# A linear-attention block mixed with a gated feed-forward block, on one core: 32 bytes of space behind each buffer of the x forms and of the gate/up weights

## The chip, the cores and the metric

The kernel runs on one core of one Trainium2 chip. The metric is the device time in microseconds (us) of one execution; 2% is what counts as faster or slower.

## The reference

The input `x` has 2048 tokens of width 640. Two branches read it, and a gate per token mixes them:

```
g   = sigmoid((x * gate_w).sum(-1))
# branch A: linear attention, 32 heads of 20
q, k, v = split(x @ wqkv)
phi(t)  = where(t > 0, t + 1, exp(t)) + 1e-6
kv  = einsum("bhsd,bhse->bhde", phi(k), v);  z = phi(k).sum over tokens
a   = (phi(q) @ kv / (phi(q) . z + 1e-6)) @ wo
# branch B: gated linear unit, 640 -> 1536 -> 640
b   = (sigmoid(x @ w_gate) * (x @ w_up)) @ w_down
out = g * a + (1 - g) * b
```

All of it is float32.

## The kernel before

Every float32 operand of a product is split into a high and a low part of type float32r: ScalarE copies the source into the high part (which rounds it), and VectorE subtracts the high part from the source. A product then takes three matmuls, high by high, high by low and low by high; the helper `mm3` records them, and in the profile they stand on lines 407, 408 and 409. The helper `act` is line 420, the helper `vec2` is line 424, `vec3` line 428, and the DMAs are issued on line 364, whatever they are for.

Block products are done with seven block multiplications in place of eight, so both `x` and the weights are needed as plain blocks and as sums of blocks. These are the **forms**: of `x` the plain ones `xa`, `xb` and the sums `xt`, of the weights `wg`, `wu` and `ws`. In tile names a last `h` or `l` is the high or the low part (`xth`, `xtl`).

The program has two stages.

- **First stage** (to about 140 us): k of all tokens, in four chunks of 512 tokens, and the sums over tokens of phi(k) and `x`. The forms of `x` are 256 columns wide there and are the stationary operand; the moving operands are the k weights (`k1h`, `ksh` and others, 322 columns) and phi(k) (`pkh`, `pkl`, 320 columns, with `xnh`, `xnl` stationary). `xnh`, `xnl`, `pkh` and `pkl` have six buffers each of 2576 bytes per partition, laid out 2592 bytes apart. Forms of `x`, k weights and staging tiles lie in the pool `pa` on the right side of the memory.
- **Second stage**: the q product and the feed-forward block, once for each pair of 512-token groups, over 12 slices of the 1536 hidden columns, with the down product in between, and at the end the attention output. Here the forms of `x` are 512 columns wide and are the moving operand; the weight forms `wg` (of 2 x 640 columns), `wu` (2 x 384) and `ws` (2 x 1152), high and low in one tile, are stationary. The first pair makes the weight forms and stores them to DRAM from GpSimd's queue, the second loads them back on SP's queue. At the end of the kernel the same buffers hold forms of phi(q) (`pl`, `pq`, `pt`, `p3`).

The instructions of all engines are put in order at build time by a planner (class `Order`), which keeps estimates of when TensorE, ScalarE and VectorE come free and fills in work that is due; the queues then run in the order written. Memory is allocated by pools: `px` holds the forms of `x` (tag `x2`, ten buffers of 2 x 512 columns; tag `x3`, four of 3 x 512), `pg` the `wg` buffers (two), `pz` one `ws` buffer and ahead of it the staging tile `xz`, `pw` the other `ws`, the `wu` buffers (two), and work tiles of 512 columns (tags `t` and `c`). `pw2` lies below `pw` and has, besides its tiles, an unused tile `room` of 256 columns that fills up the side. A pool made with `reuse_waits="tile"` lets a tile that lies where older tiles lay wait for just those.

In the built program all the tiles of the second stage that are named above begin 480 bytes past a multiple of 512 bytes: their sizes are multiples of 512 bytes per partition. In the first stage the forms of `x` begin at 160 modulo 512, and the other operands lie spread: `k1h` at 160, `k1l` 192, `k2h` 224, `k2l` 256, `ksh` 288, `ksl` 352, `k5h` 416, `k5l` 192, and the six buffers of `xnh` at 288, 320, 352, 384, 416 and 448, of `pkh` at 160 to 320 in steps of 32, likewise `xnl` and `pkl`.

Of the kernel before, what the change touches and what calls it, by code (L numbers as in the profile page):

```python
# [7 lines left out]
F32 = mybir.dt.float32  # L8
F32R = mybir.dt.float32r
# [5 lines left out]
P = 128  # L15
S, D, F = 2048, 640, 1536
# [3 lines left out]
TG = 512  # L20
# [3 lines left out]
CW = 256  # L24
# [350 lines left out]
def gated_mix_kernel(ctx: ExitStack, tc: tile.TileContext, xt, xn, wk, wv, wo, wst_q, wst_f, out_t):  # L375
# [10 lines left out]
    def f32(ap):  # L386
        return ap.bitcast(F32)
# [95 lines left out]
    def m1_tile(tag, name, dt=F32, rows=P):  # L483
        return m1.tile([rows, D], dt, name=name, tag=tag, bufs=2 if tag == "ma" else 3)
# [10 lines left out]
    for _ in range(8):  # L495
        nc.tensor.matmul(wps, warm[:, :P], warm, start=True, stop=True)

    class XForms:

        def __init__(self, pool, cols):  # L500
            def pair(n, name):
                return [pool.tile([P, n, cols], F32R, name=f"x{name}{c}", tag=f"x{n}", bufs=10 if n == 2 else 4)
                        for c in "hl"]
            self.fa, self.fr, self.fb = pair(2, "a"), pair(3, "r"), pair(3, "b")
            self.ft = [pair(2, "t") for _ in range(4)]

# [271 lines left out]
    def queue_qw(u):  # L778

        raw = qs.tile([P, 2, D], F32, name="qraw", tag="qraw")  # L780
        sp.dma_start(raw, wst_q[:, u:u + 2])
        g, v = raw[:, 0], raw[:, 1]
        w = 2 * P

        def piece(i, c, src):
            n = width(src)

            def fn():
                t = qs.tile([P, 2, w], F32R, name="qp", tag="qp", bufs=2)
                split(t[:, 0, :n], t[:, 1, :n], src)  # L790
                order.then(lambda: sp.dma_start(w_dram["q", u, i][:, :, c:c + n], f32(t[:, :, :n])))
            order.add(a_cost(n), v_cost(n), fn, "qw",
                      None, kept=True)

        for i, n in enumerate((D, 3 * P, 9 * P)):
            w_dram["q", u, i] = dram.tile([P, 2, n], F32, name=f"wq{u}{i}")
        for i, src, c0 in ((0, g, 0), (1, v, w)):
            for c in range(c0, D, w):
                piece(i, c - c0, src[:, c:min(c + w, D)])
        a11, a12, a21, a22 = g[:, :w], g[:, w:2 * w], v[:, :w], v[:, w:2 * w]  # L800
        g5, v5 = g[:, 2 * w:], v[:, 2 * w:]

        def sums(part):
            if part == 0:
                add(a22, a21, a22)
                sub(a21, a11, a21)
            else:
                sub(a11, a22, a11)
                sub(a12, a12, a11)
                sub(g5, g5, v5)  # L810
        for part in range(2):
            order.add(0, 2 * v_cost(w), lambda part=part: sums(part), "qw", None, kept=True)
        for n, t in ((7, a22), (0, a11), (5, a21), (2, a12), (4, g5)):
            piece(2, n * P, t)
# [4 lines left out]
    def tok(b, side):  # L819

        pr, j = divmod(b, 4)
        return (2 * pr + side) * 4 + j
# [14 lines left out]
    def queue_xn(b):  # L837
        for n in (2 * b, 2 * b + 1):
            order.add(a_cost(D), v_cost(D), lambda n=n: split_xn(n), ("xn", b), lambda n=n: xn_st[n][1])
# [248 lines left out]
    for c in range(1, 4):  # L1088
        ck = chunks[c]
        if c == 1:  # L1090
            queue_qw(2)
        a, b = KBlock(2 * c), KBlock(2 * c + 1)
        for n in range(1, 6):
            order.need((ck, n))
            if c == 1 and n >= 3:
                order.need(("ks", (1, 0, 2)[n - 3]))
            getattr(a, f"s{n}")()
            getattr(b, f"s{n}")()
            for _ in range(({1: 1, 2: 1, 3: 1, 5: 1}, {3: 2, 4: 2, 5: 2})[c - 2].get(n, 0) if c > 1 else 0):
                order.run("qw")  # L1100
        order.need((ck, 6))
        if c == 1:
            order.need(("ks", 5))
        if c == 2:
            chunks[c + 1].load()
        elif c == 3:
            nx = [Chunk(1, i, None, i * CW, xst_v, (b12h, b12l)) for i in range(2)]
            nx[0].load()
        if c == 1:
            order.need(("xn", 1))  # L1110
        queue_xn(2 * c)
        a.s6()
        a.s7()
        a.sum_b()
        a.phi_a()
        b.s6()
        a.phi_b()
        order.need(("pk", 2 * c - 1))
        k_split(tok(2 * c, 0))
        b.s7()  # L1120
        b.sum_b()
        k_split(tok(2 * c, 1))
        if c == 3:
            order.need("qw")
            qs_cm.__exit__(None, None, None)
            pa_cm.__exit__(None, None, None)
            px_cm = tc.tile_pool(name="px", bufs=1, side="right", reuse_waits="tile")
            px = px_cm.__enter__()
            xf = XForms(px, TG)
            pg_cm = tc.tile_pool(name="pg", bufs=1, side="right", reuse_waits="tile")  # L1130
            pg = pg_cm.__enter__()
            pz_cm = tc.tile_pool(name="pz", bufs=1, side="right", reuse_waits="tile")
            pz = pz_cm.__enter__()
            z = pz.tile([P, 8, CW], F32, name="xz", tag="ws")
            z0 = m1_tile("ma", "xm")[:, :2 * CW].rearrange("p (k c) -> p k c", c=CW)
            nx[1].x = (Rows((0, 2, z0), (2, KC, z[:, 0:3])), z[:, 3:8])
            nx[1].load(((0, 0, 2), (0, 2, KC), (1, 0, KC)))
            W, WT = {}, {}

            def wg_tile():  # L1140
                return pg.tile([P, 2, D], F32R, name="wg", tag="wg", bufs=2)

            def put(n, i, t):
                WT[n, i] = t
                W[n, i] = [t[:, c] for c in range(2)]

            def store_w(n, i):

                key = n[::2] + (i,)
                w_dram[key] = dram.tile(list(WT[n, i].shape), F32, name="w%s%d%d" % key)  # L1150
                gp.dma_start(w_dram[key], f32(WT[n, i]))

            def wg_split(n, src):
                put(n, 0, wg_tile())
                split(*W[n, 0], src)
                if n[0] == "f" or n[2] == 0:
                    order.then(lambda: store_w(n, 0))
            nx[0].f = nx[1].f = xf
            put(("q", 1, 2), 0, wg_tile())
            sp.dma_start(f32(WT[("q", 1, 2), 0]), w_dram["q", 2, 0])  # L1160
        g = GTBatch(c, batches[c])
        if c > 1:
            order.need(("xn", 2 * c))
        if c == 1:
            chunks[1].store_t(1, 0)
        elif c < 3:
            chunks[c + 1].queue()
        else:
            queue_xn(7)
        for u in range(6 if c == 1 else 4):  # L1170
            g.part(u, 0, 2, ("rot", "dd", "ch", "cc")[u % 4])
            if c == 1 and u == 0:
                order.need(("xn", 2))
                chunks[1].store_t(2, 3)
                chunks[2].queue()
            if u == (c == 1):
                b.phi_a()
            if u == 1 + (c == 1):
                b.phi_b()
                order.ahead(5)  # L1180
        queue_split(2 * c + 1)
        if c < 3:
            queue_xn(2 * c + 1)
        else:
            w_stage = m1_tile("ma", "w0")
            sp.dma_start(w_stage, wst_q[:, KC - 1])
            queue_forms(nx)
        for u in range(2 * KC):
            g.part(u, 2 if u in g.ps else 0, len(g.tiles),
                   ("rot", "dd", "rot", "cc")[u % 4] if c == 3 or u < 8 else "rot")  # L1190
            order.fill()
            if u in (3, 5, 7, 9,):
                order.run("qw")
            if c == 2 and u == 9:
                queue_ls()
# [18 lines left out]
    pw = pw_cm.__enter__()  # L1214
    pw2_cm = tc.tile_pool(name="pw2", bufs=1, side="right", reuse_waits="tile")
    pw2 = pw2_cm.__enter__()

    pw2.tile([P, 2, D], F32, name="wst", tag="wst", bufs=2)
    pw2.tile([P, 2, TG], F32R, name="hf", tag="hf2")
    pw2.tile([P, 256], F32, name="room")  # L1220

    def tt(name, dt=F32, shape=(P, TG)):
        return pw.tile(list(shape), dt, name=name, tag="t", bufs=4)
# [2 lines left out]
        return pw.tile(list(shape), dt, name=name, tag="c", bufs=5)  # L1226

    def wu_tile():
        return pw.tile([P, 2, 3 * P], F32R, name="wu", tag="wu", bufs=2)

    ws_n = []

    def ws_tile():
        ws_n.append(0)
        return (pz if len(ws_n) % 2 == 0 else pw).tile([P, 2, 9 * P], F32R, name="ws", tag="ws")

    def load_form(n, i):
        t = (wg_tile, wu_tile, ws_tile)[i]()
# [1251 lines left out]
    PL, PQ, BL, OMG, MHL = {}, {}, {}, {}, {}  # L2490

    def x2_tile(name="pl", dt=F32):
        return px.tile([P, 2, TG], dt, name=name, tag="x2", bufs=10)

    def x3_tile(name, dt=F32):
        return px.tile([P, 3, TG], dt, name=name, tag="x3", bufs=4)

    def load_m(i):

# [507 lines left out]
```

## Time and profile before

| | |
|---|---|
| median of two runs | 724.53 us (724.12 and 724.94) |
| profiled execution, first to last instruction | 722.5 us |
| lying around the span, against the median | 2.0 us |
| TensorE busy, matmuls | 718.2 us (99%), 3539 |
| TensorE weight loads | 616.7 us (85%) |
| VectorE busy | 587.1 us (81%) |
| ScalarE busy | 370.0 us (51%) |
| GpSimd busy | 114.0 us (16%) |
| DMA | 191.31 MB, 265 GB/s |

The profile is of one execution, and its own time is given by the span alone. Weight loads run beside matmuls, so the two shares of TensorE don't add up. In the rows below PE is TensorE, PEld its weight loads, DVE VectorE, ACT ScalarE, POOL GpSimd and SP SyncE, which only issues DMAs. A row of a group names the line, the engine, the operation, out<-in by tile names and shapes, the count, and then busy us and mean ns of one. The duration of a matmul (389 ns for 512 columns) contains its way through the array; matmuls overlap, and the pace is the distance between two starts.

### The profile page before, as it was taken

How to read it: one execution, taken by the hardware profiler on the slowest of the kernel's cores; microseconds unless marked ns; L12 is line 12 of the kernel's file. 1: busy time of each engine (PE TensorE's matmuls, PEld its weight loads, DVE VectorE, ACT ScalarE, POOL GpSimd, SP SyncE). 2: the span in 40 equal slices, each digit the busy share in tenths (PEclk: the TensorE clock that was granted, in tenths of full speed). 3: DMA queues.
4: the chain of work that ended last, by engine and by line, in shares of the span. 5: the costliest groups of instructions: out<-in, count | busy, mean ns of one | idle time of the engine just before them, and what ended most of it. 6: DMA issues, size and time to landing. Idle time of an engine off the chain costs nothing.

```text
span 722.5 us, 10190 instructions
## 1 busy us (share of the span) xinstructions
PE 718.2 (99%) x3539; PEld 616.7 (85%) x3539; DVE 587.1 (81%) x1028; ACT 370.0 (51%) x686; POOL 114.0 (16%) x184
## 2 busy tenths in 40 slices
PE   9999999999999999999999999999999999999998
PEld 8999999988888888888888888888888888888886
DVE  6898888988677989898989977447696968799895
ACT  6884748367556654545364664354423242454451
POOL 0211112113311212111210224001010101002200
PEclk9999999999999999999999999999999999999999
DMA  7677689598787866757687899968989895959947
GB/s 258 162 230 182 179 196 286 129 357 280 273 303 259 325 241 234 262 221 264 244 321 273 255 313 360 404 222 292 364 256 309 247 395 182 407 217 332 217 101 240
DMA packets 81690, 191.31 MB, mean 265 GB/s; under 512 B 12154, under 2 KB 40202, under 8 KB 77926
## 3 DMA queue, kind: packets, MB, share of 16 engines
q1 hardware_dynamic: 60726, 117.72, 49.6%
q0 software_dynamic: 20624, 72.70, 30.2%
q8 instruction: 28, 0.46, 0.3%
q10 hardware_dynamic: 288, 0.23, 0.1%
q14 instruction: 24, 0.20, 0.1%
HBM read 113.14 MB, written 75.20 MB: 261 GB/s over the span
## 4 chain that ended last, share of the span: by engine, by line
PE 99%; DMA 0%; DVE 0%; ACT 0%; issue 0%
PE ch L407 11%; PE ch L409 11%; PE ch L408 11%; PE cc L409 9%; PE cc L407 9%; PE cc L408 9%; PE dd L407 7%; PE dd L408 7%; PE dd L409 7%; PE rot L407 5%; PE rot L408 5%; PE rot L409 5%; PE rot L1578 1%; PE dd L2735 1%; PE ch L2735 0%; DMA xnh<-wk 0%
## 5 line engine op out<-in xcount | busy, mean ns | idle before, releaser
L420 ACT ACTIVATE c<-ch 128x512 f32<-128x512 f32 x54 | 32.3, 597 | 84.2 <-PE ch L409 83.4
L424 DVE TENSOR_TENSOR hf<-c,hf 128x512 fp32r<-128x512 f32 x80 | 54.4, 687 | 19.3 <-ACT hf L420 18.9
L420 ACT ACTIVATE hf<-c 128x512 fp32r<-128x512 f32 x80 | 48.9, 624 | 31.1 <-DVE c L424 31.0
L424 DVE TENSOR_TENSOR c<-cc,c 128x512 f32<-128x512 f32 x42 | 28.9, 688 | 28.3 <-PE cc L409 17.4
L407 PE MATMUL ch<-xth,ws 128*128 128x512 f32 x112 | 43.6, 389 | 0.0
L408 PE MATMUL ch<-xtl,ws 128*128 128x512 f32 x112 | 43.6, 389 | 0.0
L409 PE MATMUL ch<-xth,ws 128*128 128x512 f32 x112 | 43.6, 389 | 0.0
L424 DVE TENSOR_TENSOR c<-c,c 128x512 f32<-128x512 f32 x52 | 35.7, 687 | 3.3 <-ACT c L420 2.7
L424 DVE TENSOR_TENSOR tb<-rot,tb 128x512 f32<-128x512 f32 x56 | 36.1, 682 | 0.3 <-PE rot L409 0.3
L407 PE MATMUL dd<-xrh,wg 128*128 128x512 f32 x90 | 35.2, 391 | 0.0
L408 PE MATMUL dd<-xrl,wg 128*128 128x512 f32 x90 | 35.1, 390 | 0.0
L409 PE MATMUL dd<-xrh,wg 128*128 128x512 f32 x90 | 35.0, 389 | 0.0
L420 ACT ACTIVATE c<-dd 128x512 f32<-128x512 f32 x22 | 13.1, 596 | 41.4 <-PE dd L409 41.4
L407 PE MATMUL cc<-xbh,ws 128*128 128x512 f32 x84 | 32.7, 389 | 0.0
L408 PE MATMUL cc<-xbl,ws 128*128 128x512 f32 x84 | 32.7, 389 | 0.0
L409 PE MATMUL cc<-xbh,ws 128*128 128x512 f32 x84 | 32.7, 389 | 0.0
L424 DVE TENSOR_TENSOR tb<-dd,tb 128x512 f32<-128x512 f32 x36 | 24.7, 686 | 9.3 <-PE dd L409 9.2
L420 ACT ACTIVATE dd<-ch 128x512 f32<-128x512 f32 x22 | 12.8, 582 | 35.9 <-PE ch L409 35.9
L424 DVE TENSOR_TENSOR tb<-cc,tb 128x512 f32<-128x512 f32 x36 | 24.5, 684 | 1.9 <-PE cc L409 1.9
L424 DVE TENSOR_TENSOR wst<-wst 128x256 f32<-128x256 f32 (+1 forms) x65 | 24.6, 396 | 1.4
L409 PEld LDWEIGHTS ch<-xth,ws 128*128 128x128 f32 x112 | 21.0, 188 | 4.7 <-DVE ws L424 0.3
L408 PEld LDWEIGHTS ch<-xtl,ws 128*128 128x128 f32 x112 | 21.0, 188 | 4.3
(703 smaller groups left out, 2378.9 us busy)
## 6 DMA issues: line engine op xcount, KB each, us to landing
wf<-ws POOLq DMA_DIRECT2D x12, 1152.0 KB, 7.5
ws<-wf SPq DMA_DIRECT2D x11, 1152.0 KB, 8.8
wst<-wst_f SPq DMA_DIRECT2D x12, 640.0 KB, 4.9
wf<-wg POOLq DMA_DIRECT2D x12, 640.0 KB, 6.1
wd<-wd POOLq DMA_DIRECT2D x12, 640.0 KB, 8.1
wg<-wf SPq DMA_DIRECT2D x12, 640.0 KB, 6.9
wf<-wd SPq DMA_DIRECT2D x10, 640.0 KB, 11.0
xnst<-xn SPq DMA_DIRECT2D x16, 320.0 KB, 4.5
```

Of the source, the lines that this page charges most:

```text
L407: nc.tensor.matmul(out, l_hi, r_hi, start=first, stop=False, skip_group_check=True)
L408: nc.tensor.matmul(out, l_hi, r_lo, start=False, stop=False, skip_group_check=True)
L409: nc.tensor.matmul(out, l_lo, r_hi, start=False, stop=last, skip_group_check=True)
L420: nc.scalar.activation(out, src, fn, **kw)
L424: nc.vector.tensor_tensor(out, a, b, op=op)
L1578: nc.tensor.matmul(ps[:w, :w], v[:, m, :w], gt[:, m, c0:c0 + w], start=(m == 0), stop=(m == KC - 1))
L2735: nc.tensor.matmul(ps, l, r, start=new, stop=j == 1 and k == ks[-1], skip_group_check=True)
```

## The change

A helper `spaced` allocates a tile with 8 more columns (32 bytes) than it uses and returns a view without them. The second stage's forms of `x` (`x2`, `x3`), the weight forms `wg`, `wu` and `ws`, and the tiles that later take these buffers are allocated with it; `xz` gets the size of the `ws` that follows it. The pads take 640 bytes per partition, and `room` gives 640 back (256 to 96 columns).

```
+    def spaced(pool, n, cols, dt, name, tag, bufs, space=8):
+        t = pool.tile([P, n * cols + space], dt, name=name, tag=tag, bufs=bufs)
+        return t[:, :n * cols].rearrange("p (a b) -> p a b", a=n)
...
-                return [pool.tile([P, n, cols], F32R, name=f"x{name}{c}", tag=f"x{n}", bufs=10 if n == 2 else 4)
-                        for c in "hl"]
+                return [spaced(pool, n, cols, F32R, f"x{name}{c}", f"x{n}", 10 if n == 2 else 4,
+                               8 if cols == TG else 0) for c in "hl"]
...
-            z = pz.tile([P, 8, CW], F32, name="xz", tag="ws")
+            z = spaced(pz, 8, CW, F32, "xz", "ws", 1, 2 * 9 * P + 8 - 8 * CW)
...
-                return pg.tile([P, 2, D], F32R, name="wg", tag="wg", bufs=2)
+                return spaced(pg, 2, D, F32R, "wg", "wg", 2)
...
-    pw2.tile([P, 256], F32, name="room")
+    pw2.tile([P, 96], F32, name="room")
...
-        return pw.tile([P, 2, 3 * P], F32R, name="wu", tag="wu", bufs=2)
+        return spaced(pw, 2, 3 * P, F32R, "wu", "wu", 2)
...
-        return (pz if len(ws_n) % 2 == 0 else pw).tile([P, 2, 9 * P], F32R, name="ws", tag="ws")
+        return spaced(pz if len(ws_n) % 2 == 0 else pw, 2, 9 * P, F32R, "ws", "ws", 1)
...
-        return px.tile([P, 2, TG], dt, name=name, tag="x2", bufs=10)
+        return spaced(px, 2, TG, dt, name, "x2", 10)
...
-        return px.tile([P, 3, TG], dt, name=name, tag="x3", bufs=4)
+        return spaced(px, 3, TG, dt, name, "x3", 4)
```

Where the buffers begin, in bytes modulo 512, in the two built programs:

| buffers | before | after |
|---|---|---|
| `x2` (ten) | 480 each | 32, 64, 96 and on in steps of 32 to 320 |
| `x3` (four) | 480 each | 352, 384, 416, 448 |
| `wg` (two) | 480, 480 | 480, 0 |
| `wu` (two) | 480, 480 | 384, 416 |
| `ws` (in `pw`, in `pz`) | 480, 480 | 352, 448 |
| `t` and `c` (nine), not padded | 480 each | 448 each |
| four work tiles (tag `c2`) and one `hf`, not padded | 480 each | 352 each |

The high and the low part of one weight form lie in one tile and keep their distance; those of an `x` form lie in two buffers and now differ. Both programs have the same instructions in the same order on every engine, and the same waits but for three.

On SP's queue, near the end of the first stage, `xz` is loaded. These are the rows before (DMAHW and DMASW are semaphores of DMAs, the engines' names those of engines):

```order
L364 DMA xm<-xt 128x2x256 [waits DMAHW5_49,DVE_49]
L364 DMA xz<-xt 128x3x256 [waits DMASW7_49,DMAHW6_49,DMASW6_49,DMAHW7_49,DMASW5_49,DMASW4_49]
L364 DMA xz<-xt 128x5x256
L364 DMA wg<-wq_500 128x1280 [waits DMAHW0_49,PE_49]
L364 DMA w_1578<-wst_q 128x640 [waits DMAHW1_49,DVE_49]
```

and now:

```order
L364 DMA xm<-xt 128x2x256 [waits DMAHW5_49,DVE_49]
L364 DMA xz<-xt 128x3x256 [waits DMASW7_49,DMASW6_49,DMAHW6_49,DMASW5_49,DMAHW7_49,DMASW4_49,PE_49]
L364 DMA xz<-xt 128x5x256
L364 DMA wg<-wq_500 128x1280 [waits DMAHW0_49,PE_49]
L364 DMA w_1578<-wst_q 128x640 [waits DMAHW1_49,DVE_49]
```

The load of `xz` waits for TensorE too: the wider tile reaches over the start of the first stage's `xah`.

On ScalarE, early in the second stage, products of the q and feed-forward forms are copied out of PSUM (`ch`) into work tiles of tag `c`. Before:

```order
L420 ACTIVATE woh<-wo_sb 100x640 [waits DMAHW4_49]
L420 ACTIVATE c_2042<-ch_1851 128x512 [waits PE_49]
L420 ACTIVATE qe<-c_1859 128x512
L420 ACTIVATE c_1859<-c_1859 128x512 [waits Activation_49]
L420 ACTIVATE ms<-dd_2054 120x320 [waits PE_49]
L420 ACTIVATE ms<-dd_2061 120x320 [waits PE_49]
L420 ACTIVATE woh<-wo_sb 100x640 [waits DMAHW5_49]
L420 ACTIVATE c_2107<-ch_1851 128x512 [waits DMASW1_49,PE_49]
```

and now:

```order
L420 ACTIVATE woh<-wo_sb 100x640 [waits DMAHW4_49]
L420 ACTIVATE c_2042<-ch_1851 128x512 [waits DMASW1_49,PE_49]
L420 ACTIVATE qe<-c_1859 128x512
L420 ACTIVATE c_1859<-c_1859 128x512 [waits Activation_49]
L420 ACTIVATE ms<-dd_2054 120x320 [waits PE_49]
L420 ACTIVATE ms<-dd_2061 120x320 [waits PE_49]
L420 ACTIVATE woh<-wo_sb 100x640 [waits DMAHW5_49]
L420 ACTIVATE c_2107<-ch_1851 128x512 [waits PE_49]
```

The wait for a DMA out of the first stage's `kr` or `kb` tiles has moved from the later copy to the earlier one, since another of the `c` buffers is the first to lie over them.

## The prediction

> **What bounds the kernel now.** I read the page from the top: the share of busy time, the slices, then the chain that ended last.
>
> ```profile
> span 722.5 us, 10190 instructions
> PE 718.2 (99%) x3539; PEld 616.7 (85%) x3539; DVE 587.1 (81%) x1028; ACT 370.0 (51%) x686; POOL 114.0 (16%) x184
> PE   9999999999999999999999999999999999999998
> PEclk9999999999999999999999999999999999999999
> PE 99%; DMA 0%; DVE 0%; ACT 0%; issue 0%
> ```
>
> TensorE is busy for 718.2 of 722.5 us, in every slice, at full granted clock, and the chain is TensorE from end to end: no transfer and no other engine has a share. A busy TensorE can still run below its best pace, so the next view is the table of stretches (busy time and count of each engine):
>
> ```profile
> 0.00:20.00 20.00, 19.00 (x112) 16.43 (x113) 13.69 (x33) 12.94 (x31) 1.08 (x5) 1.00 0.80 263
> 20.00:135.00 115.00, 115.00 (x782) 115.00 (x782) 99.17 (x189) 74.21 (x150) 21.51 (x23) 1.00 0.74 196
> 135.00:200.00 65.00, 65.00 (x349) 56.33 (x349) 52.63 (x103) 40.05 (x72) 14.95 (x27) 1.00 0.85 280
> 200.00:410.00 210.00, 210.00 (x925) 172.79 (x924) 185.07 (x327) 113.71 (x209) 37.95 (x66) 1.00 0.76 272
> 410.00:700.00 290.00, 290.00 (x1280) 239.85 (x1279) 222.87 (x359) 124.50 (x220) 38.55 (x63) 1.00 0.86 288
> 700.00:722.50 22.50, 19.19 (x99) 16.28 (x97) 13.68 (x22) 4.55 (x8) 0.00 (x0) 1.00 0.67 210
> ```
>
> The only idle time of TensorE is 1.0 us in the first stretch and 3.3 us in the last (the final copy and store). The fullest neighbour is VectorE between 200 and 410 us: 185.07 of 210, that is 88%.
>
> Now the pace: the distance from one matmul's start to the next, by stretches of one width. The count of a stretch includes the two matmuls (one in the last row) that had begun before it; taking them off leaves the number of steps.
>
> ```profile
> 420.00:540.00 120.00, 120.00 (x531) 1.00 0.89 315
> 179.42:715.21 535.79, 535.79 (x2362) 1.00 0.82 280
> 80.96:98.41 17.45, 17.45 (x121) 1.00 0.77 177
> 64.96:80.81 15.85, 15.85 (x110) 1.00 0.50 131
> 715.44:718.91 3.47, 3.47 (x30) 1.00 0.47 170
> ...
> 419.99 0.39 PE L409 MATMUL cc<-xth,ws 128*128 128x512 f32 x1
> 539.90 0.39 PE L407 MATMUL cc<-xbh,wu 128*128 128x512 f32 x1
> 80.96 0.31 PE L407 MATMUL rot<-pkh,xnh 128*128 128x320 f32 x1
> 80.81 0.31 PE L409 MATMUL cc<-k5h,xbl 128*128 128x322 f32 x1
> 718.91 0.28 PE L409 MATMUL rot<-hf,wf 128*128 128x256 f32 x1
> ```
>
> From 419.99 to 539.90 are 529 steps of 512 columns: 119.91/529 = **226.7 ns**. Over the whole 512-column stretch, 535.79/2360 = 227.0 ns. The 320-column stretch of the first stage gives 17.45/119 = 146.6 ns, the 322-column one 15.85/107 = 148.1 ns, the 256-column end 3.47/29 = 119.7 ns. So the long stretch runs within 0.3 ns of its own best part: 0.3 × 2360 = 0.8 us is all that TensorE loses there to waits of any kind.
>
> **The change part by part.** No instruction is added, removed or reordered on any engine; the order rows show three waits that differ. What moves is where tiles lie. So the price has three parts: those waits, the pace of TensorE with the new starts, and the durations on VectorE, ScalarE and the DMAs.
>
> *The waits.* The load of `xz` now also waits for TensorE, because the wider tile reaches 320 bytes into where the first stage's `xah` lay. The instructions that still held that place:
>
> ```profile
> 99.91 0.19 PEld L408 LDWEIGHTS ch<-k1l,xah 128*128 128x128 f32 x1
> 115.71 1.46 SPq L364 DMA_DIRECT2D xz<-xt  x2
> 160.13 0.60 ACT L420 ACTIVATE c<-ch 128x512 f32<-128x512 f32 x1 [0.33 <-PE ch L409]
> 132.89 1.19 POOL L364 DMA_DIRECT2D zacc<-kb  x1 [3.45 <-DVE gt L424]
> zacc<-kb POOLq DMA_DIRECT2D x8, 320.0 KB, 5.5
> ```
>
> TensorE's last read of `xah` begins at 99.91 us, and the load is issued at 115.71: the wait is met long before, by up to 15.8 us. Even if it weren't, behind it on SP's queue stand the second half of `xz` and the loads of `wg`, `w0` and `wst`, and the forms made from `xz` would come late for TensorE. The DMA wait that goes from one copy to `c` (166.25 us) to an earlier one (160.13 us) is for a store out of `kr` or `kb`; the last of those is issued at 132.89 and lands 5.5 us later, 22 us ahead of the copy. Both cost 0; ScalarE's copy waits for TensorE anyway, as its row says.
>
> *VectorE and ScalarE.* The trace holds the comparison that the change makes: in the first stage the six-buffer tiles (`xnh`, `xnl`, `pkh`, `pkl`) lie 32 bytes further modulo 512 from one buffer to the next, in the second stage all lie at 480. Same operation, same 640 columns:
>
> ```profile
> L424 DVE TENSOR_TENSOR xnl<-xnst,xnh 128x640 fp32r<-128x640 f32 x15 | 11.8, 821 | 0.3
> L424 DVE TENSOR_TENSOR wg<-wst,wg 128x640 fp32r<-128x640 f32 x13 | 10.7, 821 | 5.4 <-ACT wg L420 5.4
> L424 DVE TENSOR_TENSOR wd<-dst,wd 128x640 fp32r<-128x640 f32 x12 | 9.8, 819 | 0.0
> L420 ACT ACTIVATE xnh<-xnst 128x640 fp32r<-128x640 f32 x16 | 11.1, 730 | 0.0
> L420 ACT ACTIVATE wg<-wst 128x640 fp32r<-128x640 f32 x13 | 9.5, 729 | 1.4 <-PE dd L409 1.4
> L420 ACT ACTIVATE wd<-dst 128x640 fp32r<-128x640 f32 x12 | 8.4, 727 | 0.0
> ```
>
> 821 ns spread out, 821 and 819 ns at one offset; ScalarE 730 against 729 and 727. The effect is between nothing and 0.4%, of either sign. On VectorE's 185.07 us that is 0.7 us, hidden below TensorE, which has 25 us more to do in that stretch; without that cover it would be the whole 0.7. VectorE would set the pace only if its operations grew by 13%.
>
> *TensorE.* Between the 256-column end and the 512-column stretch, both with operands at one offset, lie (226.7 − 119.7)/256 = 0.418 ns per column. This puts 320 columns at 146.4 ns and 322 at 147.3. The first stage, with its spread operands, measures 146.6 and 148.1: 0.2 and 0.8 ns more. From 135 us on there are 349 + 925 + 1280 + 99 = 2653 matmuls, so the spread costs between **0.5 and 2.1 us** if those differences are its doing. Downwards the bound is what TensorE's weight loads wait for other engines after the first 7 us:
>
> ```profile
> PEld ch L409 <- DVE ws L424: 0.3, 2, 0.2
> PEld rot L407 <- ACT rot L420: 0.3, 1, 0.3
> PEld cc L407 <- DVE tb L424: 0.2, 1, 0.2
> PEld dd L407 <- ACT dd L420: 0.2, 1, 0.2
> PEld dd L408 <- DVE xrl L424: 0.2, 1, 0.2
> PEld ch L407 <- ACT cx L420: 0.2, 1, 0.2
> ```
>
> That is 1.4 us in all, so the change is worth between −1.4 and +2.1 us here. I take 0: the 320-column stretch is the one whose tiles lie as the change lays them, in steps of 32 bytes, and its 0.2 ns is no more than the reading error of the 256-column stretch (0.01 us over 29 steps is 0.3 ns).
>
> *The DMAs.* The pads aren't transferred, so packets and bytes stay. A slower transfer would show only where an engine of the chain waits for one, and TensorE never does.
>
> **The sum.** 722.5 + 0 (waits) + 0 (VectorE, ScalarE, DMAs) + 0 (TensorE) = 722.5 us of span. The median of the two runs, 724.53, lies 2.0 us above the span; with these 2.0 the forecast is **724.5 us**, no change.
>
> **The rivals.**
> *Contention goes.* If buffers at one offset slow VectorE or ScalarE when TensorE reads beside them, spreading them takes away waits. At most 1.4 us is there to be had: 723.1. Against it: the equal rows of 640 columns. For it: VectorE's 88% leaves the 0.2 us waits as the places where a late result shows. The Trainium skill, page "SBUF — State Buffer", section "SBUF: two separate sides", says that inside the engine side only the port pair shared by VectorE and GpSimd contends; by that rule the gain is nothing and the time 724.5, and the rows of 640 columns agree.
>
> *Slower: TensorE's stream pays for its start.* The moving operands in the second stage are the forms `x2` and `x3`, and each matmul reads one from its start or from 2048 bytes on. If an operand that begins off the old common offset costs one more fetch, each of the 2653 matmuls pays; by the 322-column stretch 0.8 ns, which is 2.1 us: 726.6. It decides over the 2% only from 14.5/2653 = 5.5 ns per matmul on, seven times that price. Against it: the 320-column stretch shows 0.2. The Trainium skill, page "Advanced Engine Details and Errata", section "SBUF Cachelines", says that SBUF is read in lines of 16 bytes and that crossing lines costs. By that rule a start moved by 32 bytes costs nothing here and the time is 724.5, since every second slice of 322 columns begins 8 bytes into a line (1288 = 80 × 16 + 8) while every start of the change is a whole line; no run here separates the two.
>
> *The layout doesn't move.* The moved waits show that it does.
>
> **How the numbers follow.** Forecast (no change within the runs' spread) 0.72; contention goes 0.12; TensorE pays 0.13; something that no row shows 0.03, of it 0.01 faster and 0.02 slower by over 2%. The range takes in both rivals, with half of the 0.8 us between the two runs (724.12 and 724.94) on each side: 723.1 − 0.4 to 726.6 + 0.4, so 722.7 to 727.0. Two per cent, 14.5 us, is about what a measurement of this kernel tells from no change. Faster by more: 0.01; within: 0.97; slower by more: 0.02.
>
> **What would show it.** After the change the stretch from 420 to 540 us should again hold 531 matmuls (226.7 ns); 530 or fewer means that TensorE pays. The 640-column rows of `wg` should read 821 and 729 again, the waits of the weight loads 1.4 us in sum, the chain 99% TensorE. The forecast is wrong if the matmul pace moves by a nanosecond, if VectorE's operations grow towards 13%, or if TensorE begins to wait at `xz`'s forms near 125 us.

## The result, and the profile after

The changed kernel takes 734.91 us (734.88 and 734.95), against 724.53 us before: a ratio of 1.0142 with a 95% interval of 1.0125 to 1.0158. That is 10.4 us slower, short of the 2% and far outside the range of 722.7 to 727.0. The page after, its share of busy time, TensorE's slices and the chain that ended last:

```profile
span 733.1 us, 10190 instructions
PE 729.0 (99%) x3539; PEld 617.5 (84%) x3539; DVE 587.8 (80%) x1028; ACT 370.4 (51%) x686; POOL 114.1 (16%) x184
PE   9999999999999999999999999999999999999998
PEclk9999999999999999999999999999999999999999
PE 99%; DVE 0%; ACT 0%; issue 0%
```

This could be the page of before: the same instructions, TensorE busy for 99%, at full granted clock, alone in the chain. Only its busy time has grown, from 718.2 to 729.0 us, which is the whole difference. VectorE (587.1 to 587.8), ScalarE (370.0 to 370.4) and GpSimd (114.0 to 114.1) have stayed. So no other engine sets the time; TensorE does the same matmuls at a slower pace. The table of stretches (busy time and count of TensorE, its weight loads, VectorE, ScalarE and GpSimd; granted clock, DMA share, GB/s) says where:

```profile
20.00:135.00 115.00, 115.00 (x782) 115.00 (x781) 99.15 (x189) 74.17 (x150) 21.42 (x23) 1.00 0.74 196
135.00:200.00 65.00, 65.00 (x346) 55.64 (x345) 52.00 (x102) 39.55 (x71) 14.97 (x27) 1.00 0.85 279
200.00:410.00 210.00, 210.00 (x911) 170.44 (x909) 181.98 (x320) 110.55 (x201) 38.01 (x66) 1.00 0.74 267
410.00:711.00 301.00, 301.00 (x1301) 243.87 (x1300) 228.11 (x367) 129.13 (x228) 38.59 (x63) 1.00 0.85 281
```

The first stage, up to 135 us, has its 782 matmuls in 115.00 us as before. Then the loss is even. Between 135 and 200 us 346 matmuls stand where 349 stood, and between 200 and 410 us 911 where 925 stood; the last long stretch needs 301 us for 1301 − 2 steps, 231.7 ns each, where before 290 us held 1280 − 2, 226.9 ns each. By stretch the loss is 3 × 0.2 = 0.6 us, 14 × 0.23 = 3.2 us and 1299 × 4.8 ns = 6.2 us: 10.0 of the 10.6 us between the spans. The two stretches that the prediction named for its own test, of the 512-column matmuls of the second stage and the 320-column ones of the first:

```profile
420.00:540.00 120.00, 120.00 (x520) 1.00 0.88 310
80.87:98.32 17.45, 17.45 (x121) 1.00 0.74 182
```

520 in place of 531; the 320 columns as before, 119 steps in 17.45 us. The costliest group of matmuls (instructions | busy us, mean ns of one | idle) before,

```profile
L409 PE MATMUL ch<-xth,ws 128*128 128x512 f32 x112 | 43.6, 389 | 0.0
```

and after, with the rows of 640 columns that the prediction wanted to see again, the load of `xz`, and the whole list of what the weight loads waited for:

```profile
L409 PE MATMUL ch<-xth,ws 128*128 128x512 f32 x112 | 44.2, 395 | 0.0
L424 DVE TENSOR_TENSOR wg<-wst,wg 128x640 fp32r<-128x640 f32 x13 | 10.7, 820 | 6.0 <-ACT wg L420 6.0
L420 ACT ACTIVATE wg<-wst 128x640 fp32r<-128x640 f32 x13 | 9.5, 730 | 1.5 <-PE dd L409 1.5
L364 SPq DMA_DIRECT2D xz<-xt x2: 373/464/556, 115.4 to 115.8; - x2
...
PEld L496 <- issue: 2.5, 7, 0.8
PEld ch L1027 <- ACT xah L420: 0.7, 1, 0.7
PEld rot L407 <- ACT rot L420: 0.3, 1, 0.3
```

One matmul of this group takes 395 ns instead of 389. It overlaps the next one, so the extra 6 ns go with the slower pace: in the first experiment below, 389 goes with a pace of 226.7 ns and 395 with 233.3. VectorE's and ScalarE's rows read 820 and 730 ns, against 821 and 729 before. `xz` is issued at 115.4 us, not held up. Of the 1.4 us of short waits 0.3 us are left, which fits a TensorE that comes later itself.

Which operand goes with which pace? In the built programs every matmul's moving operand (a slice of an `x` form or of a work tile) and its weights have a known address. Before, all 512-column matmuls read both from the same offset modulo 256 bytes. After, 758 of the 2489 have a distance of 0 (8 of them are the warm-up at the start, whose operands are one constant), and the others lie apart by 32 (251), 64 (224), 96 (323), 128 (224), 160 (164), 192 (325) or 224 bytes (220). Weights are loaded while a matmul streams: in the trace before, the load for the matmul of 500.23 us runs from 500.01 to 500.20, beside the matmul that began at 500.01. That made the first theory of the experiments: what counts is the *distance* between the start of the moving operand and that of the weights that are read beside it.

### The profile page after: what moved, and what is told of

It is laid out like the page before. It is cut to its first block, busy times and chain, and to the rows that moved or that the text cites. A ratio compares the mean times of both kernels' runs of the same rounds, so it can differ in the third digit from the quotient of the medians.

```text
span 733.1 us, 10190 instructions
## 1 busy us (share of the span) xinstructions
PE 729.0 (99%) x3539; PEld 617.5 (84%) x3539; DVE 587.8 (80%) x1028; ACT 370.4 (51%) x686; POOL 114.1 (16%) x184
## 4 chain that ended last, share of the span: by engine, by line
PE 99%; DVE 0%; ACT 0%; issue 0%
PE ch L407 11%; PE ch L409 11%; PE ch L408 11%; PE cc L407 9%; PE cc L409 9%; PE cc L408 9%; PE dd L409 7%; PE dd L407 7%; PE dd L408 7%; PE rot L407 5%; PE rot L409 5%; PE rot L408 5%; PE rot L1583 1%; PE dd L2740 1%; PE rot L496 0%; PE ch L2740 0%
```

## The experiments

**The pace by itself, by distance.** A new kernel runs blocks of 60 matmuls in the kernel's own pattern (high with high, high with low, low with high parts) on one tile of moving operands and one of weights, and shifts the slices by a number of bytes. These lines, shortened, say how, with some of the blocks:

```
+ m = mv[:, 512*j + mh : 512*j + mh + w];  s = sw[:, c + wh : c + wh + 128]   # mh, wh: bytes/4
+ block("same", at(0), at(0))            # no shift
+ block("m32x", at(32), at(0))           # moving operand 32 bytes on
+ block("both32x", at(32), at(32))       # both
+ block("mwspr", spread, spread_w)       # each buffer elsewhere
+ block("samevecx", at(0), at(0), work=224)   # with work on VectorE and ScalarE at another offset
```

> This kernel leaves the whole computation out: it is a row of blocks of 60 float32r matmuls each (128 x 128 weights), one after the other, with no other engine at work but in the three blocks whose names end in vec or vecx. A block's PSUM tile has its name: same = moving operand and weights begin at one offset modulo 512 bytes; m32x = moving operand 32 bytes further than the weights; both32x = both 32 further; ml32x = only the low part of the moving operand 32 further; wl32x = only the low part of the weights; mspr, wspr, mwspr = moving operand, weights, both at offsets that change by group; numbers 256x to 448x at the end are widths. Theory A (the offset between the moving operand and the weights loaded beside it sets the pace): same and both about 226.7 ns per 512 columns, m32x and others above it, up to the 231.4 ns of the changed kernel; mspr, wspr, mwspr about 231. Theory B (a change of offset from one matmul to the next costs, a constant offset doesn't): same, both and every m..x 226.7; ml, wl, mspr, wspr, mwspr 229 to 233. Theory C (other engines' reads and writes collide with TensorE's): every block without vector work 226.7, those with it 229 to 233. Theory D (the absolute start): both32x above same. If the cost grows with the columns, mwspr256x is at or below same256x (119.7) and mwspr448x some 3 ns above same448x.

The timeline of this kernel (start in us, duration, operation) with the first matmul of four blocks that follow one another:

```profile
26.39 0.39 PE L71 MATMUL same<-mv,sw 128*128 128x512 f32 x1
39.99 0.40 PE L71 MATMUL m32x<-mv,sw 128*128 128x512 f32 x1
54.00 0.40 PE L71 MATMUL m64x<-mv,sw 128*128 128x512 f32 x1
67.74 0.40 PE L71 MATMUL m96x<-mv,sw 128*128 128x512 f32 x1
```

60 steps without a shift take 13.60 us, **226.7 ns** each; with the moving operand 32 bytes on 14.01 us, 233.5; with 64 bytes 13.74 us, 229.0. The first few steps of a block still differ, so the paces that follow, here and in the other kernels of this kind, are counted from a block's seventh matmul to its last: 233.3 for 32 bytes and 228.8 for 64. The groups of the same kernel, where the means of one matmul move with the pace:

```profile
L71 PE MATMUL m64x<-mv,sw 128*128 128x512 f32 x60 | 13.9, 392 | 0.0
L71 PE MATMUL ml64x<-mv,sw 128*128 128x512 f32 x60 | 14.1, 394 | 0.0
L71 PE MATMUL m256x<-mv,sw 128*128 128x512 f32 x60 | 13.8, 389 | 0.0
L71 PE MATMUL both32x<-mv,sw 128*128 128x512 f32 x60 | 13.8, 390 | 0.0
L71 PE MATMUL mwspr<-mv,sw 128*128 128x512 f32 x60 | 14.0, 393 | 0.0
L71 PE MATMUL samevecx<-mv,sw 128*128 128x512 f32 x60 | 13.8, 389 | 0.0
L71 PE MATMUL same320x<-mv,sw 128*128 128x320 f32 x60 | 9.0, 309 | 0.0
L71 PE MATMUL mwspr320x<-mv,sw 128*128 128x320 f32 x60 | 9.0, 309 | 0.0
L71 PE MATMUL same256x<-mv,sw 128*128 128x256 f32 x60 | 7.4, 283 | 0.0
L71 PE MATMUL mwspr256x<-mv,sw 128*128 128x256 f32 x60 | 7.2, 280 | 0.0
```

What the starts are by themselves does not count: moved together by 32 bytes, moving operand and weights run at 227.1 ns (226.65 over the last 20 steps). What another engine does beside it does not count either: `samevecx` stays at 226.66 ns. Moved against each other the pace is 233.3 to 233.4 ns at 32, 96, 128, 192, 384 and 480 bytes, 228.8 at 64, and 226.66 at 256. With the weights moved alone by 32 bytes it is 233.4. Where every buffer lies elsewhere (`mwspr`), as after the change, it is 231.2. A mixture is not the mean of its parts: with only the low part of the moving operand 64 bytes on (`ml64x`), so that distances 0 and 64 alternate, the pace is 232.1, slower than either alone (226.7 and 228.8). And the price depends on the width: the spread costs 4.5 ns at 512 columns and 2.5 at 384 (173.3 to 175.8), 0.15 at 320 (146.68 to 146.83), and at 256 and 448 it *gains* 2.1 (120.0 to 117.9) and 2.8 (206.7 to 203.9). That gain was not expected: a cost that grows with the columns would have made 448 columns slower. So the theories of the absolute start (D) and of the other engines (C) fall, and so does theory B, by which a constant distance is free; what holds is that the distance counts, modulo 256. With the paces of this run the distances of the changed kernel come to 224 × 2.2 ns + 1507 × 6.7 ns = 10.6 us (taking 6.7 for 160 bytes too, which this run did not have), which is the measured total; whether it holds matmul by matmul comes at the end.

**Half of the change: the `x` forms alone.** Their helper and pads stay, everything else lies as before (a filler keeps the other pools in place).

```
+            px.tile([P, 16], F32, name="fill")
...
-        return px.tile([P, 2, TG], dt, name=name, tag="x2", bufs=10)
+        return spaced(px, 2, TG, dt, name, "x2", 10)
...
```

> Only the forms of x get their 32 bytes; weight forms and all work tiles stay at 480. Theories A and B: about 60% of the 512-column matmuls stream such a form, so 6 to 9 us of the 10.4 us, about 732 us. Theory C: the same if it is the forms that VectorE and ScalarE write, else nothing (724.5). Theory D: half of the forms lie at 0 modulo 64, half at 32: up to 5 us.

734.86 us against 724.67: 1.0136 (1.0114 to 1.0158), 10.2 us; the sum over its distances is 10.0. The stretch from 420 to 540 us:

```profile
420.00:540.00 120.00, 120.00 (x520) 1.00 0.89 311
```

**The other half: the weight forms alone.** The `ws` in `pz` still begins at 480, so 1230 of the 2489 matmuls keep the distance 0.

```
...
-        return pw.tile([P, 2, 3 * P], F32R, name="wu", tag="wu", bufs=2)
+        return spaced(pw, 2, 3 * P, F32R, "wu", "wu", 2)
...
```

> Only the weight forms get their 32 bytes (wg at 416 and 448, wu at 416 and 448, the ws of pw at 384); forms of x and work tiles stay at 480. Theory A: the offset between moving operand and weights is not 0 for nearly all matmuls with x forms: 6 to 9 us, about 732 us. Theory B: high and low part keep their distance within a tile, so offsets change only from form to form: 1 to 3 us, about 726.5 us. Theory C: 724.5 us, or a part of the 10 us for writes of weight forms.

732.51 us: 1.0103 (1.0084 to 1.0122), 7.8 us where the sum over the distances gives 6.5. The same stretch:

```profile
420.00:540.00 120.00, 120.00 (x522) 1.00 0.88 310
```

Either half costs most of the whole, and 10.2 + 7.8 is not 10.4: once the two streams lie apart, moving the other one as well adds next to nothing. Two independent prices would have added up. The weights, which no theory of the moving operand alone would have charged, cost 7.8 us by themselves; theory B's 1 to 3 us miss that.

**No spread, only an offset: all `x` forms 32 bytes on.** All fourteen buffers keep one common offset. If it were the spread from buffer to buffer, nothing would be lost.

```
+            px.tile([P, 8], F32, name="fill")
...
+            px.tile([P, 120], F32, name="filler")
...
-    pw2.tile([P, 256], F32, name="room")
+    pw2.tile([P, 128], F32, name="room")
```

> No pads between the forms of x: all of them are moved by 32 bytes together, from 480 to 0 modulo 512; weights and work tiles stay at 480. Theory A: the offset between moving operand and weights is a constant 32 for the x forms: several us, about 730 us. Theory B: offsets change only between products of x forms and those of hf: 0 to 2 us, about 725.5 us. Theory C: 724.5 us or little more. Theory D: the start at 0 instead of 480 is what costs: 5 us or more.

737.22 us: 1.0168 (1.0149 to 1.0187), 12.5 us, the dearest of all. 1781 matmuls read an `x` form, and 1781 × 6.67 ns are 11.9 us. The stretch and the group:

```profile
420.00:540.00 120.00, 120.00 (x518) 1.00 0.87 309
...
L409 PE MATMUL ch<-xth,ws 128*128 128x512 f32 x112 | 44.2, 395 | 0.0
```

**A finer sweep of the distance, at five widths.** The first kernel again, with 36 matmuls in a block.

```
+ for o in (0, 4, 8, 12, 16, 20, 24, 28, 32, 40, 48, ..., 224, 240, 256):
+     block(f"m{o}x", at(o), at(0), 512, 36)
```

> This kernel leaves the whole computation out: blocks of 36 matmuls with a constant distance between the start of the moving operand and that of the weights, m32x for 32 bytes, at 512 columns; n320m32x the same at 320 columns, n322.., n256.., n448... If only the distance modulo 256 counts, m0x and m256x give 226.7 ns, m64x 228.8, and 32, 96, 128, 192 give 233.3 to 233.4. Open: distances that are no multiple of 32 (4 to 48), and whether some distance is faster than 0; at 320 columns spread operands gave steps of 140 to 154 ns around a mean of 146.8, so if the pace of 320 columns also belongs to a distance, constant blocks lie at single values between 140 and 154, and one of them below the 146.7 of distance 0. If the distance doesn't matter at 320 columns, all of n320 read 146.7.

```profile
L71 PE MATMUL m0x<-mv,sw 128*128 128x512 f32 x36 | 8.3, 389 | 0.0
L71 PE MATMUL m20x<-mv,sw 128*128 128x512 f32 x36 | 8.8, 402 | 0.0
L71 PE MATMUL m32x<-mv,sw 128*128 128x512 f32 x36 | 8.6, 395 | 0.0
L71 PE MATMUL m64x<-mv,sw 128*128 128x512 f32 x36 | 8.6, 397 | 0.0
L71 PE MATMUL m240x<-mv,sw 128*128 128x512 f32 x36 | 8.3, 388 | 0.0
L71 PE MATMUL n320m0x<-mv,sw 128*128 128x320 f32 x36 | 5.4, 309 | 0.0
L71 PE MATMUL n320m32x<-mv,sw 128*128 128x320 f32 x36 | 5.4, 309 | 0.0
L71 PE MATMUL n320m80x<-mv,sw 128*128 128x320 f32 x36 | 5.7, 317 | 0.0
```

At 512 columns no distance beats 226.7 ns: 0 and 240 reach it, 256 comes back to it after its first steps (227.0 as counted here, 226.7 over the last 20), 28 takes 227.8, 12 takes 228.9, and most others 231 to 234, up to 239.5 at 20. At 320 columns 12 of 14 distances take 146.6 to 146.7 ns; 16 takes 145.3 and 80 takes 153.3. At 322 they lie between 146.7 and 149.3, at 256 between 117.8 and 120.0, at 448 between 199.9 (64 bytes) and 206.7 (0). So at 448 columns, distance 0 is the slowest of the five tried. One thing is new: 64 bytes take 233.3 ns here and 228.8 in the first kernel, with the same slices. What ran just before differs, so the pace seems to depend on history too.

**Back to a whole period: all `x` forms 256 bytes on.** The edit is that of 32 bytes, with 64 columns ahead and 64 behind:

```
+            px.tile([P, 64], F32, name="fill")
...
+            px.tile([P, 64], F32, name="filler")
```

> All forms of x moved by 256 bytes together (from 480 to 224 modulo 512), weights and work tiles at 480. If the distance modulo 256 sets the pace: no cost, 724.5 to 725.0 us. If the distance modulo 512, or the common start at 480, counts: about 737 us as with 32 bytes.

724.41 against 724.44 us: 0.9999 (0.9989 to 1.0009). The same tiles have moved, the same work lies over other old tiles, and nothing is lost, though modulo 512 the offset is another:

```profile
420.00:540.00 120.00, 120.00 (x531) 1.00 0.88 313
...
L409 PE MATMUL ch<-xth,ws 128*128 128x512 f32 x112 | 43.6, 389 | 0.0
```

**64 bytes on.** With 16 columns ahead and 112 behind.

```
+            px.tile([P, 16], F32, name="fill")
...
+            px.tile([P, 112], F32, name="filler")
```

> All forms of x moved by 64 bytes together (from 480 to 32 modulo 512). By the distance, 1781 matmuls with such forms at 228.8 instead of 226.7 ns: 3.8 us, about 728.4 us. If any distance but 0 costs the same: about 737 us.

731.00 us: 1.0091 (1.0076 to 1.0107), 6.6 us, where 4 were expected. Spread over the 1781 that is 3.7 ns each, between the 2.1 of the first kernel and the 6.6 of the sweep, but that is not where it is lost. With every matmul of this run's trace from 200 us on sorted by its distance in the built program, 1576 steps at distance 64 take 229.5 ns, 2.6 more than before and near the first kernel's price, while the 669 at distance 0, which have not moved, take 230.3, 3.4 more. So a third of the loss falls on matmuls that the sum took for free.

```profile
420.00:540.00 120.00, 120.00 (x524) 1.00 0.87 310
```

**Whose weights, and for how long?** While a matmul streams, the weights of the next one are loaded. A third kernel gives each matmul its own shifts: `own32x` shifts every second matmul's moving operand with its own weights, `next32x` with the weights of the one that follows; `one12x` shifts the moving operand of one matmul in twelve; `then64x` begins with three others.

```
+ row("own32x",  lambda k: 32 * (k % 2), lambda k: 32 * (k % 2))
+ row("next32x", lambda k: 32 * (k % 2), lambda k: 32 * ((k + 1) % 2))
+ row("one12x",  lambda k: 32 * (k % 12 == 11), none)
+ row("after64x", lambda k: 64, none)
```

> This kernel leaves the whole computation out. Blocks of 72 matmuls of 512 columns. own32x: the moving operand and the weights of the same matmul move by 32 bytes together in every second matmul, so that a matmul's distance to its own weights is always 0 and to the weights of the next matmul, which are loaded while it streams, always 32. next32x: the reverse (distance to its own weights 32, to the next ones 0). If the load of the next weights beside the stream is what matters: own32x, own96x, own128x at 231 to 234 ns, next at 226.7. If a matmul's own weights matter: the reverse. If both or neither: equal. one4x to one24x: one matmul in 4, 8, 12, 24 is moved by 32 bytes; a cost that stays with this matmul gives 6.7 ns divided by 4, 8, 12, 24 on the mean pace (228.3, 227.5, 227.2, 226.9), a disturbance that lasts for some ten matmuls keeps one4x, one8x and one12x near 230 to 232. after64x and then64x differ only in the three first matmuls (distance 96): the same pace if the distance alone sets it, another if the pace also depends on how the stretch began, as the 228.8 and 233.3 for 64 bytes in two kernels suggest.

```profile
L98 PE MATMUL calm<-mv,sw 128*128 128x512 f32 x72 | 16.5, 389 | 0.0
L98 PE MATMUL own32x<-mv,sw 128*128 128x512 f32 x72 | 16.9, 394 | 0.0
L98 PE MATMUL next32x<-mv,sw 128*128 128x512 f32 x72 | 16.7, 392 | 0.0
L98 PE MATMUL one12x<-mv,sw 128*128 128x512 f32 x72 | 16.8, 393 | 0.0
L98 PE MATMUL one24x<-mv,sw 128*128 128x512 f32 x72 | 16.6, 391 | 0.0
L98 PE MATMUL after240x<-mv,sw 128*128 128x512 f32 x72 | 17.0, 396 | 0.0
```

The expectation that one of the two would be free missed: matched to its own weights a row takes 231.7 ns, matched to the next one's 230.0, both above the calm 226.7. Nor is one of them always the slower: at 96 bytes they take 234.0 and 229.9, at 128 bytes 228.3 and 230.0. And a single shifted matmul does not cost 6.7 ns. In `one24x` the shifted matmul and the nine behind it take 2320 ns (from 345.44 to 347.76 us, and again from 350.93 to 353.25) where ten calm ones take 2267; then the pace is back. That is 53 ns for one, and the same 53 in `one12x`; with one in 8 or in 4 shifted, where the next comes before the pace is back, it is 30 and 23 ns each on average. The history counts at one distance, but not always. `then64x`, `then28x` and `then16x`, which begin with three matmuls at 96 bytes, run like `after64x` (228.9), `after28x` (226.7) and `after16x` (231.6), within 0.2 ns. But 240 bytes take 233.3 ns in `after240x` and 236.7 in `then240x`, and took 226.7 in the sweep, where the slices come in another order. Once the first matmuls of a block are past, only distance 0 (or 256) gives 226.7 wherever it was tried without others mixed in.

**Everything at another common offset.** The whole right-hand side of the memory lies 32 bytes off, so nearly all moving operands and weights move together; some 250 matmuls read one side from a tile that stays where it was.

```
+            px.tile([P, 8], F32, name="fill")
...
-    pw2.tile([P, 256], F32, name="room")
+    pw2.tile([P, 248], F32, name="room")
```

> Forms of x, weight forms and work tiles of the right side all moved by 32 bytes together, from 480 to 448 modulo 512; tiles of the left side (most hf, wf, wd, ds) stay. 2239 of the 512-column matmuls keep the distance 0, 250 (those of a right-side and a left-side operand) get 32 or 224. If the distance between the two operands sets the pace: 250 x 6.7 ns = 1.7 us, about 726.2 us. If what counts is where the operands start, or that work tiles and forms lie apart: as with the forms of x moved by 32, about 737 us.

728.90 against 724.29 us: 1.0062 (1.0045 to 1.0079), 4.6 us. The theory that a start off the old offset costs asked for 737. The distance theory, at 6.7 ns for each of the 250, asked for 726.2, and is off as well; 4.6 us over 250 are 18 ns each, which fits a disturbance that lasts, as in the last experiment, and not a price of 6.7 that stays with the matmul.

```profile
420.00:540.00 120.00, 120.00 (x528) 1.00 0.88 312
```

Sorted by distance in this run's trace, from 200 us on, the 243 mixed steps take 233.1 ns, and the 2026 at distance 0 take 228.3, where before they took 226.9: 2.8 of the 4.6 us are lost by matmuls that have not moved against their weights at all. No run moved every tile together, so that a common offset is free is shown by the first kernel alone. The changed kernel shows the same: there 737 steps at distance 0 take 229.8 ns, the others 231.3 to 233.6, and the mean over all is 231.3, which is what the spread block of the first kernel gave (231.2). So the sum by constant distances (10.6 us) is right in total by luck: it takes the matmuls at distance 0 for free, which cost 2.9 ns each in the changed kernel, and charges the others 6.1 ns on average, where they cost 5.2.

## Why the prediction was wrong, point by point

*What bounds the kernel* was right: TensorE from end to end before and after, and nothing else late.

*The waits* were right. `xz` is issued at 115.4 us and TensorE is busy for all of 115.00 us up to 135 us.

*VectorE and ScalarE* were right: 820 and 730 ns for 640 columns, as before.

*The DMAs* were right: nothing of the chain waits for one.

***TensorE*** is the step that failed, by its term of 0 us with bounds of −1.4 and +2.1. Measured, this term is 10.6 us of the span, all of it TensorE's pace. The prediction compared the spread operands of the first stage with a line drawn through 256 and 512 columns, read 0.2 and 0.8 ns, and carried these to the second stage as a price per matmul. At 320 columns the line was good: 146.4 by it, 146.68 measured at distance 0. The step to 512 columns was not. The price of a spread changes sign with the width, −2.1 ns at 256, 0.15 at 320, 2.5 at 384, −2.8 at 448 and 4.5 at 512, and 320 columns, the width that the trace had, is where it is near nothing. At 322 columns the 0.8 ns were no price of a spread at all: the sweep takes 148.4 ns there at distance 0, more than the 148.1 of the first stage, so it was the line (147.3) that was off. Two slips there change nothing: 0.3 × 2360 ns is 0.7 us and not 0.8, and 107 steps are right by the starts in the trace, though 110 less two is 108. A row of another width was taken for a row of the same thing. Nor was there any row of before with the spread at 512 columns: all of them lay at one offset modulo 512, so the trace could not have shown the price, and a bound from the nearest rows was no bound.

*The slower rival*, a price on every matmul of the second stage, was right as to where and in kind, and it too was mis-sized: 0.8 ns were put in, and 231.3 − 226.9 = 4.4 ns came out, over some 2400 steps 10.6 us. It took the `x` forms for the moving operand of all 2653 matmuls, where 1781 read one. It was also wrong as to the cause: not an operand's start, but its distance to the weights, which the prediction named nowhere. Its 5.5 ns for the 2% were not reached. *Contention goes* had 1.4 us to gain; 1.1 us of those waits are indeed gone, but in a kernel that is slower, which fits a TensorE that comes later itself and no gain.

Two rules of the Trainium skill bear on this point, and both would have the change cost nothing. The Trainium skill's page "Advanced Engine Details and Errata", section "SBUF Cachelines", speaks of 16-byte lines, and by it a shift of 32 bytes, two whole lines, should be free. At 512 columns it took 233.3 ns against 226.7. The Trainium skill's page "TensorE: Matmul & The Clock Gate", section "Step-by-step: what each phase is for", says that TensorE has two independent read ports, so that loading the next weights takes no read bandwidth from the running matmul. Here nothing but the distance between the two streams was changed: 32 bytes cost 6.7 ns in the first kernel and 256 bytes nothing, in its block and in the whole run. On what the change costs the measurement decides; whether the loads take read bandwidth it does not show.

What stays open is why. The trace shows starts and durations of matmuls and weight loads, not their single reads, so that two streams get in each other's way is argued, and that the pace depends on their distance modulo 256 bytes, on the width and on the matmuls shortly before is shown. Nor is it shown what in the history counts. Other distances for the first stage's 322 columns (148.1 ns now, 146.7 at the best distances of the sweep) could be worth an estimated 444 × 1.4 ns, 0.6 us, which is within the spread of the runs; it was not tried.

The prediction also took 2%, 14.5 us, for about what a measurement of this kernel tells from no change. The interval of 1.0125 to 1.0158 shows that far less can be told.

## What to carry to other kernels

Where TensorE bounds a kernel, look at the addresses of a matmul's two operands: with 512 float32r columns, moving operand and weights at the same offset modulo 256 bytes ran at 226.7 ns, and most other distances 1 to 6% slower, without a wait in the profile. A common offset for all buffers is therefore not a conflict to be spread out but, for this width, the best layout found; a matmul out of line also slows those behind it. And a price read at one shape holds for that shape alone: where the trace has no row of the operation as the change will run it, the range has to say so.

## What the runs showed of the hardware that was not expected

- The pace of back-to-back float32r matmuls, each with its own weights, depends on where the two operands lie relative to each other: 226.7 ns at distance 0 and 256, 233.3 at 32, 239.5 at 20 bytes (512 columns). Moved together by 256 bytes or by 32, they keep 226.7 after the first few matmuls.
- The same spread is a gain at 256 and 448 columns, by 2.1 and 2.8 ns, and at 448 columns a distance of 64 bytes took 199.9 ns against 206.7 at 0.
- One matmul out of line by 32 bytes costs 53 ns, spread over itself and the nine behind it, and not the 6.7 ns of a constant distance. In the whole kernel, matmuls at distance 0 among others took 228 to 230 ns instead of 226.9.
- A page that is the same in every share (99% busy, full clock, no waits) hid a loss of 1.4%; TensorE's busy time in us (718.2 to 729.0), counts in equal windows and the mean of one matmul (389 to 395 ns) showed it.
